# One core, attention and two MLP blocks: attention units of later batches at a lower rank, and the tails of the second block loaded and split earlier

## The chip, the core and the metric

The kernel runs on one NeuronCore of a Trainium2 chip. A core has TensorE (PE, matmuls; its weight loads are listed apart as PEld), VectorE (DVE), ScalarE (ACT), GpSimd (POOL) and SyncE (SP), which issues nearly all of the DMA transfers here. Each engine works through its own list of instructions in the order of the program and waits on semaphores of the others. The metric is the device time of one execution in microseconds (us).

## What is computed

Attention with rotary embedding over 4 batches, 8 heads, 576 positions and head width 64, then an MLP block with a norm, then a gated MLP block. Cut to what matters:

```python
# q, k, v: (4, 8, 576, 64) float32; rotate() is the rotary embedding
q_rot, k_rot = (rotate(q), rotate(k))
scores = scale * np.matmul(q_rot, k_rot.transpose(0, 1, 3, 2))
scores = scores - np.max(scores, axis=-1, keepdims=True)
attn = np.exp(scores)
attn = attn / (np.sum(attn, axis=-1, keepdims=True) + 1e-09)
x = np.matmul(attn, v)                      # then (4, 576, 512)

# first block, d_model 512, hidden 2048
xn = (x - mu) / np.sqrt(var + 1e-06) * g_ln
x = x + np.maximum(xn @ w_ch1, 0.0) @ w_ch2

# second block, d_ff 1024
h = gelu_tanh(x @ w_in)
u, v = (h[..., :512], h[..., 512:])
v_n = (v - mu) / np.sqrt(var + 1e-06) * g_ln
v_s = np.einsum('ts,bsd->btd', w_sg, v_n) + b_sg[None, :, None]
out = x + (u * v_s) @ w_out
```

## The kernel before

**Precision.** A float32 operand is cut into a high and a low part of the fast matmul type, and a product is three matmuls (high by high, low by high, high by low). A cut is a cast on ACT and a subtraction on DVE. The weights of the first block arrive as 8-byte numbers; a "conversion" of one of their 32 tiles is a scaling on ACT (L48), three bit operations on DVE (L50, L52, L55), a cast on ACT (L635) and a subtraction on DVE (L637), and the tile is then stored to a scratch area in DRAM (`wsc`, L641), from which later batches load it again.

**Attention.** The 4 batches follow each other. A batch has 16 units, 64 in all; a unit is one head and 288 of the 576 queries. A unit is: ten score matmuls into `S` (L311, in two parts, four matmuls and six); the maximum over the key chunks on DVE (`mx`, L334); the maximum over partitions on POOL (`am`, L337); then one of two ways to subtract the maximum and exponentiate. Until all 32 converted tiles are stored, five matmuls on PE add minus the maximum into `S` (L392, below "add") and ACT exponentiates out of `S` (L395); afterwards DVE subtracts (L376, `sT<-S,am`, below "subtract") and ACT exponentiates (L381). At last five float32 matmuls with the values (`PV`, L350; the trace shows ten, since each runs as two passes) and two copies on ACT. `S` exists once, so a unit's scores wait for the exponentials of the unit before.

**First block.** Beside the attention of a batch, PE works on the first block of the batch before it: `up` (L655 to L657, 12 matmuls for one output tile) and `down` (L685 to L687). Their results lie in two banks and are evacuated by ACT and DVE (`h`, L663 and L665; `acc`, L699 and L702). Between attention and first block of a batch stands its norm: DVE takes the sums of the exponentials (L477, after their transfer `sums<-sr`, L364), their reciprocal, and then `ln` matmuls on PE (L492, L508, L549) alternate with DVE and ACT. The attention results lie in 17 tiles `x0`, 8 for a batch; so the third batch's units beyond its first two must wait until the first batch's block has stored its result.

**What sets the order.** All of this is written out by a planner (`Sched`). Its tasks are Python generators that name, step by step, an engine, an earliest time and a duration. It takes the step that can start first; a step of lower rank number goes first if it could start within 0.4 of that step's duration. Units had rank 0 (0.5 once their PV runs), evacuations 1, norms 2, preparation of queries, keys and values 3 to 3.2, weight loads 3.5, conversions 4, the first block's matmuls 5. The durations are constants in the code, and the resulting order is fixed in the program.

**Second block** (`moe2`). It takes the batches in turn: `V` (L1006 to L1008, the half that is normed; 5 output tiles for an even batch, since the fifth holds the last 64 positions of two batches, the "tails"), then gelu and norm statistics, the split of the normed tiles (`w<-v`, L1023 and L1025), `U` (L1038 to L1040), the position mixing `G` (L1054 to L1058), and the output (L963 to L965). Its inputs are loaded by `load_x` (L937) and `load_tails` (L977) and split by L949, L951 and, for the tails, L981 and L983. The first batch's loads and splits are tasks of the planner, run while the last first-block work goes on (`ahead`, rank 4.5); everything behind them is ordered by the framework.

Of the kernel before, what the change touches and what calls it, by code (L numbers as in the profile page):

```python
# [20 lines left out]
KEY0 = (0, 128, 256, 384, 448)  # L21
L_CONV = 10.0
HOLD = 0.4
FG = [4, 8, 8, 4]

AHEAD = 2
# [6 lines left out]
def f32(ap):  # L33
    return ap.bitcast(F32)
# [24 lines left out]
class Sched:  # L59
# [27 lines left out]
    def run(self, until=lambda: False):  # L87
        while self.tasks and not until():
# [6 lines left out]
            for x in sorted((x for x in c if x[3]["eng"] == t["eng"] and x[1] < rank), key=lambda x: x[:3]):  # L95
                if x[0] - s < HOLD * t["us"]:
                    s, rank, _, t = x
# [27 lines left out]
def latest(*xs):  # L125

    return None if any(x is None for x in xs) else max(xs)


class Attn:  # L130
# [172 lines left out]
    def unit(self, i):  # L303
        nc, c, u = self.nc, self.c, self.units[i]
        B, j, S, g, p, hi = u["B"], u["j"], self.S, u["g"], u["p"], u["hi"]
        Kb = B["kof"]

        def scores(c0, c1):
            for ch in range(c0, c1):
                for t in range(2):  # L310
                    x = nc.tensor.matmul(S[:, ch, 0:HQ], Kb["K"][j][:, KEY0[ch]:KEY0[ch] + 128], B["X"][:, j, 1 - t, :],  # L311
                                         start=t == 0, stop=t == 1)
                    if ch < 2 and "exp" in self.last:
                        self.tc.declare_no_dep(x.ins, self.last["exp"][1].ins, reason="reads the other banks")

        yield "PE", lambda: latest(self.Sfree[0], Kb["k0"], B["q"][j], self.k["x0_free"](g, p, hi)), 0.55
        scores(0, 2)
        self.Sfree[0] = None
        e = yield "PE", lambda: latest(self.Sfree[1], Kb["k"]), 0.82
        scores(2, 5)  # L320
        self.Sfree[1] = None
        self.k["x0"](g, p, hi)
        B["left"] -= 1
        if B["left"] == 0:
            self.X.give(B["xslot"], e + 0.1)
        Kb["kusers"] -= 1
        if Kb["kusers"] == 0:
            self.K.give(Kb["kslot"], e + 0.1)
        if i + 1 < len(self.units):
            c.task(self.unit(i + 1), 0)  # L330
        self.ahead(i)
        e = yield "DVE", e + 0.35, 1.68
        mx = self.p.tile([128, HQ], F32, tag="mx", name="mx", bufs=1)
        nc.vector.tensor_reduce(mx, S[:, :, 0:HQ].rearrange("p c q -> p q c"), AX.X, ALU.max)  # L334
        e = yield "POOL", e + 0.1, 1.75
        am = self.p.tile([128, HQ], F32R, tag="am", name="am", bufs=AB)
        nc.gpsimd.partition_all_reduce(am, mx, 128, bass_isa.ReduceOp.max)  # L337
        if self.k["spare"]():
            x1, slot, sT = yield from self.subtract(am, e)
        else:  # L340
            x1, slot, sT = yield from self.add(am, e)
        V = B["vof"]
        ps = None
        for c0, c1 in ((0, 2), (2, 5)):
            e = yield "PE", (lambda: latest(x1, self.PV.free(), V["v"])) if c0 == 0 else 0.0, 0.51 * (c1 - c0), 0.5
            if c0 == 0:
                bank = self.PV.take()
                ps = self.ps.tile([128, 512], F32, tag="PV", name="PV")[:, 0:HQ]
            for ch in range(c0, c1):
                nc.tensor.matmul(ps, V["vin"][:, ch, 64 * j:64 * j + 128], sT[:, ch, :], start=ch == 0, stop=ch == 4)  # L350
        self.sT.give(slot, e)
        V["users"] -= 1
        if V["users"] == 0:
            self.vfree.give(V["vslot"], e)
        a, b = 64 * j, 64 - 64 * j
        yield "ACT", e + 0.35, 0.41
        nc.scalar.copy(self.k["x0"](g, p, hi)[a:a + 64], ps[a:a + 64])  # L357
        e = yield "ACT", 0.0, 0.41
        t = self.p.tile([128, HQ], F32, tag="sr", name="sr", bufs=1)
        nc.scalar.copy(t[b:b + 32], ps[b:b + 32])  # L360
        self.PV.give(bank, e + 0.1)
        e = yield "SP", e + 0.1, 0.6
        r = 32 * hi + 2 * p + j
        nc.sync.dma_start(out=self.sums[self.sums_of(g, hi)][r:r + 1], in_=t[b:b + 1])  # L364
        if u["ends"]:
            self.done.append(e + 3.0)
# [57 lines left out]
def fused_kernel(ctx, tc, q, k, v, cs, cst, w12, wi, wo, wsg, wsg4, gb, out):  # L424
# [163 lines left out]
    for g in range(NG):  # L588
        n = FG[g]
        for F in range(16 // n):  # L590
# [53 lines left out]
    def up(g, f, hh):  # L644
# [15 lines left out]
        def end(e=e):  # L660
            e = yield "ACT", e + 0.35, 0.43
            t = h[g, f, hh] = hpool[g].tile([128, 2, HQ], F32R, tag="h", name="h", bufs=FG[g] * 2)
            G["relu"] = nc.scalar.activation(t[:, 0, :], ps, AF.Relu).ins  # L663
# [7 lines left out]
    def down(g, F, c, hh):  # L671
        n = FG[g]
        b, halves = groups[g]
# [45 lines left out]
    def mlp_pass(g, F, halves=(0, 1), ups=None):  # L719

        n = FG[g]
        seq = [(f, hh) for f in ups or range(n) for hh in halves]
# [17 lines left out]
    def open_h(g):  # L740
        if g in hpool:
            return
        if FG[g] != hpool.get("n"):
            if g:
                hpool["ctx"].close()
            hpool["n"], hpool["ctx"] = FG[g], ExitStack()
            hpool[g] = hpool["ctx"].enter_context(tc.tile_pool(name=f"h{g}", bufs=1, side="left"))
# [63 lines left out]
    def last_group():  # L811
        wpool = pctx.enter_context(tc.tile_pool(name="w2b", bufs=1, side="right"))
        pps = pctx.enter_context(tc.tile_pool(name="ps2", bufs=6, space=PS))
        w2.rest(wpool)
        second.append(moe2(tc, M, hpool[NG - 1], wpool, pps, B, x1d, w2.t, gbt, eps, out, lambda: xn[1] == 2 * NG))
# [83 lines left out]
def moe2(tc, M, hp, wpool, pp, B, x1d, w, gbt, eps, out, through):  # L899
# [23 lines left out]

    X = {}

    def load_x(b):
        if b >= B:
            return
        x1, at = {}, {}
        xh, xl = [], []  # L930
        X[b] = (x1, xh, xl)
        for c in range(4):
            for hh in range(2):
                qs = slice(HQ * hh, HQ * hh + HQ)
                e = yield "SP", 0.0, 0.6
                x1[c, hh] = t = M.tile([128, HQ], F32, tag="x0", name="x0", bufs=17)
                nc.sync.dma_start(out=t, in_=x1d[b, c, :, qs])  # L937
                at[c, hh] = e or 0.0
        for c in range(4):
            if c == 2:  # L940
                yield "SP", lambda: 0.0 if through() else None, 0.0
            if c % 2 == 0:
                xh.append(M.tile([128, 2, 576], F32R, tag="xh", name="xh", bufs=2))
                xl.append(M.tile([128, 2, 576], F32R, tag="xl", name="xl", bufs=2))
            for hh in range(2):
                qs = slice(HQ * hh, HQ * hh + HQ)
                t, h, l = x1[c, hh], xh[c // 2][:, c % 2, qs], xl[c // 2][:, c % 2, qs]
                e = yield "ACT", at[c, hh] + 4.0, 0.42
                nc.scalar.copy(h, t)  # L949
                yield "DVE", (e or 0.0) + 0.1, 0.46  # L950
                nc.vector.tensor_tensor(l, t, f32(h), ALU.subtract)  # L951
# [20 lines left out]
    def load_tails(b):  # L972

        s = M.tile([128, 512], F32, tag="sq", name="tails", bufs=2)
        for c in range(4):
            e = yield "SP", 0.0, 0.6
            nc.sync.dma_start(out=s[:, 128 * c:128 * c + 128].rearrange("p (b q) -> p b q", b=2),  # L977
                              in_=x1d[b:b + 2, c, :, 512:576].rearrange("b p q -> p b q"))
        e = yield "ACT", (e or 0.0) + 4.0, 0.63
        tails[b] = t = M.tile([128, 2, 512], F32R, tag="w", name="w", bufs=WB)  # L980
        nc.scalar.copy(t[:, 0, :], s)  # L981
        yield "DVE", (e or 0.0) + 0.1, 0.7
        nc.vector.tensor_tensor(t[:, 1, :], s, f32(t[:, 0, :]), ALU.subtract)  # L983

    def at_once(steps):
        for _ in steps:
            pass

    yield from load_x(0)
    yield from load_tails(0)  # L990
    yield None
    for b in range(B):
        x1, xh, xl = X[b]
# [48 lines left out]
        if b:  # L1042
            final(b - 1)
        at_once(load_x(b + 1))
        if b % 2 and b + 1 < B:
            at_once(load_tails(b + 1))
        gt = {}
        for hh in range(2):
            qs = slice(HQ * hh, HQ * hh + HQ)
            for c in range(4):  # L1050
# [11 lines left out]
                g = gt[c, hh] = hp.tile([128, 2, HQ], F32R, tag="h", name="h", bufs=8)  # L1062
# [66 lines left out]
```

## Time and profile before

| | |
|---|---|
| median of three runs | 999.93 us (998.19 to 1001.24) |
| the profiled execution's own time | 1002.52 us |
| span of its trace, first to last instruction | 1000.7 us |
| PE busy / PEld busy | 939.7 us (94%) / 867.8 us (87%) |
| DVE / ACT / POOL busy | 714.2 (71%) / 444.6 (44%) / 91.4 us (9%) |
| mean granted TensorE clock | 0.985 of full speed |
| chain that ended last | PE 73%, DVE 14%, DMA 5% |

The profiled execution took 1.8 us more than its span and 2.6 us (0.26%) more than the median run. Busy time of an engine counts only executing instructions; what a matmul's end is, the profiler models, so that matmuls overlap in the rows and "busy" PE is not PE at its peak. Times below count from the start of the span.

### The profile page before, as it was taken

How to read it: one execution, taken by the hardware profiler on the slowest of the kernel's cores; microseconds unless marked ns; L12 is line 12 of the kernel's file. 1: busy time of each engine (PE TensorE's matmuls, PEld its weight loads, DVE VectorE, ACT ScalarE, POOL GpSimd, SP SyncE). 2: the span in 40 equal slices, each digit the busy share in tenths (PEclk: the TensorE clock that was granted, in tenths of full speed). 3: DMA queues.
4: the chain of work that ended last, by engine and by line, in shares of the span. 5: the costliest groups of instructions: out<-in, count | busy, mean ns of one | idle time of the engine just before them, and what ended most of it. 6: DMA issues, size and time to landing. Idle time of an engine off the chain costs nothing.

```text
span 1000.7 us, 15881 instructions
## 1 busy us (share of the span) xinstructions
PE 939.7 (94%) x6057; PEld 867.8 (87%) x6057; DVE 714.2 (71%) x1188; ACT 444.6 (44%) x901; POOL 91.4 (9%) x78
## 2 busy tenths in 40 slices
PE   4688899999998889999999999999999979999998
PEld 3566688798898778989998999999999969989998
DVE  6998666699788788865589744586553887667764
ACT  3564554665434355443235531425222546345441
POOL 1121112122000211100012110000000000000000
PEclk9899999999999899999999999999999989999999
DMA  9888444378464564653755533588763300303011
GB/s 273 240 283 263 110 106 109 104 202 258 152 207 146 189 213 134 204 163 121 251 182 145 156 128 127 192 285 273 250 204 91 90 1 12 95 2 89 1 49 48
DMA packets 93420, 153.76 MB, mean 154 GB/s; under 512 B 38048, under 2 KB 60576, under 8 KB 93344
## 3 DMA queue, kind: packets, MB, share of 16 engines
q1 hardware_dynamic: 92800, 152.16, 49.1%
q8 instruction: 48, 0.79, 0.3%
q10 hardware_dynamic: 544, 0.59, 0.2%
q14 instruction: 28, 0.23, 0.1%
HBM read 107.25 MB, written 26.21 MB: 133 GB/s over the span
## 4 chain that ended last, share of the span: by engine, by line
PE 73%; DVE 14%; DMA 5%; ACT 2%; issue 2%; POOL 2%; SPq 1%; DVEq 0%; ACTq 0%; POOLq 0%
PE PV L350 8%; PE S L311 7%; PE m L686 6%; PE m L685 6%; PE m L687 6%; PE m L655 5%; PE m L657 5%; PE m L656 5%; DVE mx L334 4%; DMA sums<-sr 3%; PE S L392 2%; PE p L1054 2%; PE p L1055 2%; PE p L1056 2%; DVE sT L376 2%
## 5 line engine op out<-in xcount | busy, mean ns | idle before, releaser
L350 PE MATMUL PV<-sT,vin 128*128 128x288 f32 x640 | 170.8, 413 | 3.6 <-ACT sr L360 1.8
L655 PE MATMUL m<-xh,w 128*128 128x288 f32 x480 | 148.0, 308 | 2.4 <-DVE h L665 2.3
L350 PEld LDWEIGHTS PV<-sT,vin 128*128 128x128 f32 x640 | 120.1, 194 | 32.7 <-ACT sr L360 2.7
L685 PE MATMUL m<-h,w 128*128 128x288 f32 x480 | 145.2, 302 | 0.0
L686 PE MATMUL m<-h,w 128*128 128x288 f32 x480 | 142.0, 296 | 0.0
L334 DVE TENSOR_REDUCE mx<-S 128x288 f32<-128x1440 f32 x64 | 106.0, 1657 | 49.9 <-PE S L311 48.8
L656 PE MATMUL m<-xl,w 128*128 128x288 f32 x480 | 141.5, 295 | 0.0
L657 PE MATMUL m<-xh,w 128*128 128x288 f32 x480 | 141.2, 294 | 0.0
L687 PE MATMUL m<-h,w 128*128 128x288 f32 x480 | 140.5, 293 | 0.0
L337 POOL PARTITION_ALL_REDUCE am<-mx x64 | 89.3, 1395 | 500.4 <-DVE mx L334 500.4
L311 PE MATMUL S<-X,K 128*128 128x288 f32 x640 | 112.6, 321 | 16.8 <-ACT X L200 10.2
L311 PEld LDWEIGHTS S<-X,K 128*128 128x128 f32 x640 | 95.5, 201 | 29.2 <-ACT sT L395 11.0
L665 DVE SCALAR_TENSOR_TENSOR h<-m,h 128x288 fp32r<-128x288 f32 x128 | 58.0, 454 | 66.6 <-ACT h L663 65.8
L655 PEld LDWEIGHTS m<-xh,w 128*128 128x128 f32 x480 | 90.0, 188 | 6.5 <-DVE h L665 3.6
L663 ACT ACTIVATE h<-m 128x288 fp32r<-128x288 f32 x128 | 52.2, 408 | 95.0 <-PE m L657 94.5
L656 PEld LDWEIGHTS m<-xl,w 128*128 128x128 f32 x480 | 90.2, 188 | 1.4
L686 PEld LDWEIGHTS m<-h,w 128*128 128x128 f32 x480 | 90.2, 188 | 1.0
L685 PEld LDWEIGHTS m<-h,w 128*128 128x128 f32 x480 | 90.0, 188 | 1.1
L657 PEld LDWEIGHTS m<-xh,w 128*128 128x128 f32 x480 | 90.3, 188 | 0.0
L687 PEld LDWEIGHTS m<-h,w 128*128 128x128 f32 x480 | 90.2, 188 | 0.0
L357 ACT COPY x<-PV 64x288 f32<-64x288 f32 x64 | 25.2, 394 | 137.8 <-PE PV L350 137.7
L395 ACT ACTIVATE sT<-S 128x576 f32<-128x576 f32 x74 | 53.6, 769 | 29.7 <-PE S L392 28.3
(149 smaller groups left out, 1848.9 us busy)
## 6 DMA issues: line engine op xcount, KB each, us to landing
w<-wsc SPq DMA_DIRECT2D x96, 512.0 KB, 4.3
X<-qin SPq DMA_DIRECT2D x124, 144.0 KB, 2.6
cd<-in_w SPq DMA_DIRECT2D x32, 512.0 KB, 6.1
wsc<-w SPq DMA_DIRECT2D x24, 512.0 KB, 3.6
qin<-in_q SPq DMA_DIRECT2D x31, 288.0 KB, 4.4
kin<-in_k SPq DMA_DIRECT2D x15, 576.0 KB, 5.0
vin<-in_v SPq DMA_DIRECT2D x40, 160.0 KB, 4.2
x1d<-x SPq DMA_DIRECT2D x32, 144.0 KB, 2.7
```

Of the source, the lines that this page charges most:

```text
L311: x = nc.tensor.matmul(S[:, ch, 0:HQ], Kb["K"][j][:, KEY0[ch]:KEY0[ch] + 128], B["X"][:, j, 1 - t, :], start=t == 0, stop=t == 1)
L334: nc.vector.tensor_reduce(mx, S[:, :, 0:HQ].rearrange("p c q -> p q c"), AX.X, ALU.max)
L337: nc.gpsimd.partition_all_reduce(am, mx, 128, bass_isa.ReduceOp.max)
L350: nc.tensor.matmul(ps, V["vin"][:, ch, 64 * j:64 * j + 128], sT[:, ch, :], start=ch == 0, stop=ch == 4)
L395: ex.append(nc.scalar.activation(sT[:, c0:c1, :], self.S[:, c0:c1, 0:HQ], AF.Exp, scale=0.125))
L655: nc.tensor.matmul(ps, w[:, 0, ms], xh[:, kc, :], start=kc == 0, stop=False)
L656: nc.tensor.matmul(ps, w[:, 0, ms], xl[:, kc, :], start=False, stop=False)
L657: nc.tensor.matmul(ps, w[:, 1, ms], xh[:, kc, :], start=False, stop=kc == 3)
L665: nc.vector.scalar_tensor_tensor(t[:, 1, :], ps, 0.0, f32(t[:, 0, :]), op0=ALU.max, op1=ALU.subtract)
L685: nc.tensor.matmul(ps, w[:, 0, ms], t[:, 0, :], start=a == 0, stop=False)
L686: nc.tensor.matmul(ps, w[:, 1, ms], t[:, 0, :], start=False, stop=False)
L687: nc.tensor.matmul(ps, w[:, 0, ms], t[:, 1, :], start=False, stop=a == n - 1)
```

## The change

Two edits. First, a unit of batch 1, 2 or 3 (counted from 0) enters the planner with rank 2.5 and no longer 0, so its scores, maximum, subtraction and exponentials stand behind evacuations (1) and norms (2) where these could start at about the same time. Units of batch 0 keep rank 0. Second, `load_tails` is cut into the loads (`load_tails`) and the split (`split_tails`); for the first batch of the second block the tails are loaded before the other inputs, and split in the middle of `load_x`, ahead of the two last chunks. For the third batch nothing changes: both halves run at once, as before.

```diff
+UNIT = (0, 2.5, 2.5, 2.5)
...
         if i + 1 < len(self.units):
-            c.task(self.unit(i + 1), 0)
+            c.task(self.unit(i + 1), UNIT[self.units[i + 1]["g"]])
...
-    def load_x(b):
+    def load_x(b, between=()):
...
             if c == 2:
                 yield "SP", lambda: 0.0 if through() else None, 0.0
+                yield from between
...
         s = M.tile([128, 512], F32, tag="sq", name="tails", bufs=2)
+        e = None
         for c in range(4):
...
+        return s, e
+
+    def split_tails(b, s, e):
         e = yield "ACT", (e or 0.0) + 4.0, 0.63
...
-    yield from load_x(0)
-    yield from load_tails(0)
+    s = yield from load_tails(0)
+    yield from load_x(0, split_tails(0, *s))
     yield None
...
         if b % 2 and b + 1 < B:
-            at_once(load_tails(b + 1))
+            at_once(split_tails(b + 1, *at_once(load_tails(b + 1))))
```

By its new ranks the planner writes another order for PE, DVE, ACT and SP from the 17th unit on, the first of the second batch; POOL's is the same. Six units fewer use the add (31, before 37) and six more the subtract (33, before 27), since the 32 conversions are now through earlier in the order. All other instructions keep their number. (Line numbers of the changed kernel are one higher up to the second block, and some nine higher in it.)

Second batch, DVE. All that stands from the maximum of the 28th unit to the one after it, before (`mx` the maximum, `qin` a query split, `ce` and `w<-ce` conversion steps):

```order
L334 TENSOR_REDUCE mx<-S 128x288
L202 TENSOR_TENSOR qin<-qin 128x288
L55 SCALAR_TENSOR_TENSOR ce<-cd,ce 128x512
L50 TENSOR_SCALAR ce<-ce 128x512
L52 SCALAR_TENSOR_TENSOR ce<-cd,ce 128x512
L637 TENSOR_TENSOR w<-ce,w 128x512
L55 SCALAR_TENSOR_TENSOR ce<-cd,ce 128x512
L334 TENSOR_REDUCE mx<-S 128x288
```

The same place on DVE in the changed kernel (`h<-m,h` evacuates a bank of the first block):

```order
L335 TENSOR_REDUCE mx<-S 128x288
L666 SCALAR_TENSOR_TENSOR h<-m,h 128x288
L203 TENSOR_TENSOR qin<-qin 128x288
L666 SCALAR_TENSOR_TENSOR h<-m,h 128x288
L51 TENSOR_SCALAR ce<-ce 128x512
L53 SCALAR_TENSOR_TENSOR ce<-cd,ce 128x512
L56 SCALAR_TENSOR_TENSOR ce<-cd,ce 128x512
L666 SCALAR_TENSOR_TENSOR h<-m,h 128x288
L638 TENSOR_TENSOR w<-ce,w 128x512
L51 TENSOR_SCALAR ce<-ce 128x512
L53 SCALAR_TENSOR_TENSOR ce<-cd,ce 128x512
L56 SCALAR_TENSOR_TENSOR ce<-cd,ce 128x512
```

Between two maxima stand now eleven other instructions where six stood: more of the conversions and of the first block's evacuations fall to one unit. On PE a unit of this batch goes with 36 matmuls of the first block, before with 18.

Third batch, PE. The start of its third and fourth unit before (`S<-X` scores, `S<-am` the add):

```order
L311 MATMUL S<-X,K_1936 128x288 x10
L392 MATMUL S<-am,e_63 128x288 x5
L311 MATMUL S<-X,K_1937 128x288 x10
L350 MATMUL PV<-sT,vin_81 128x288 x5
L392 MATMUL S<-am,e_63 128x288 x5
```

The same start on PE in the changed kernel (`ln` belongs to the second batch's norm, `m<-h` is `down` work):

```order
L312 MATMUL S<-X,K_2368 128x288 x4
L509 MATMUL ln<-lt,ones 128x288
L312 MATMUL S<-X,K_2368 128x288 x6
L686 MATMUL m<-h,wx 128x288
L687 MATMUL m<-h,wx 128x288
L688 MATMUL m<-h,wx 128x288
```

Before, nothing stood between the scores and the add that needs their maximum. Now 126 `down`, `up` and `ln` matmuls stand between these scores and the fourth unit's, and there is no add: this unit subtracts on DVE.

Second block, DVE. Around the split of the first tails before (`acc` and `x` end the last batch's first block, `sq` and `acc<-sq` are gelu steps of `U`):

```order
L920 SCALAR_TENSOR_TENSOR sq<-sq,acc 128x288
L922 SCALAR_TENSOR_TENSOR acc<-sq,acc 128x288
L710 TENSOR_TENSOR x_5540<-acc,x_5540 128x288
L983 TENSOR_TENSOR w<-tails,w 128x512
L920 SCALAR_TENSOR_TENSOR sq<-sq,acc 128x288
```

The same split on DVE in the changed kernel (`xl<-x,xh` is the split of the other inputs):

```order
L953 TENSOR_TENSOR xl<-x_7438,xh 128x288
L953 TENSOR_TENSOR xl<-x_7440,xh 128x288
L666 SCALAR_TENSOR_TENSOR h<-m,h 128x288 x2
L989 TENSOR_TENSOR w<-tails,w 128x512
L953 TENSOR_TENSOR xl<-x_7442,xh 128x288
L666 SCALAR_TENSOR_TENSOR h<-m,h 128x288
```

The split moved from behind the last batch's final additions to a place ahead of the last inputs' split. On PE the fifth `V` tile's 12 matmuls moved with it: before, 8 `U` matmuls stood between the last of them and the first `G` matmul; now 95 `U` and 24 `down` matmuls stand there.

## Rows read from the trace of the kernel before

**Rows 1.** First part of the page: busy us, share, instructions of each engine.
```profile
PE 939.7 (94%) x6057; PEld 867.8 (87%) x6057; DVE 714.2 (71%) x1188; ACT 444.6 (44%) x901; POOL 91.4 (9%) x78
```
**Rows 2.** Stretches: length, busy us (instructions) of PE PEld DVE ACT POOL, clock, DMA share, GB/s.
```profile
164.30:200.50 36.20, 34.00 (x191) 28.79 (x190) 23.47 (x30) 22.92 (x43) 7.11 (x6) 1.00 0.33 89
200.50:256.70 56.20, 55.98 (x346) 50.50 (x345) 50.28 (x69) 35.55 (x69) 12.90 (x9) 1.00 0.80 243
256.70:322.00 65.30, 63.66 (x464) 62.11 (x463) 56.47 (x116) 27.24 (x55) 1.10 (x1) 1.00 0.45 154
...
334.00:380.80 46.80, 43.74 (x260) 37.51 (x259) 36.97 (x46) 22.30 (x41) 7.97 (x7) 1.00 0.69 221
...
803.00:814.00 11.00, 3.76 (x15) 3.44 (x15) 10.53 (x25) 8.62 (x19) 0.00 (x0) 0.70 0.00 1
```
**Rows 3.** Timeline of PE, third batch's start and second batch: start, us, [idle before].
```profile
327.48 1.57 PE L392 MATMUL S<-am,e 128*128 128x288 f32 x5 [4.18 <-POOL am L337]
329.06 2.77 PE L311 MATMUL S<-X,K 128*128 128x288 f32 x10
331.63 3.19 PE L350 MATMUL PV<-sT,vin 128*128 128x288 f32 x10
...
251.78 0.82 PE L392 MATMUL S<-am,e 128*128 128x288 f32 x5
...
253.24 1.56 PE L311 MATMUL S<-X,K 128*128 128x288 f32 x10
254.63 2.59 PE L350 MATMUL PV<-sT,vin 128*128 128x288 f32 x10
```
**Rows 4.** Short stretches, same columns: third batch's start, and the second block.
```profile
328.00:330.00 2.00, 1.98 (x9) 1.63 (x7) 1.97 (x5) 1.73 (x4) 0.00 (x0) 0.50 0.00 0
...
814.00:820.00 6.00, 6.00 (x47) 6.00 (x46) 3.81 (x8) 0.87 (x2) 0.00 (x0) 0.99 0.00 0
```
**Rows 5.** Timelines of DVE, PE and ACT around the first G matmul of the second block.
```profile
795.74 0.69 DVE L983 TENSOR_TENSOR w<-tails,w 128x512 fp32r<-128x512 f32 x1
...
801.55 0.39 PE L1008 MATMUL p<-wih,w 128*128 128x512 f32 x1
...
809.57 3.34 ACT L1023 CAST w<-v 128x512 fp32r<-128x512 f32 x6 [0.84 <-DVE v L1019]
...
810.24 1.81 PE L1054 MATMUL p<-wgh,w 128*128 128x288 f32 x6 [7.24 <-ACT w L1023]
```
**Rows 6.** Groups of DVE instructions by line: busy us, mean ns, idle us before.
```profile
L334 DVE TENSOR_REDUCE mx<-S 128x288 f32<-128x1440 f32 x64 | 106.0, 1657 | 49.9 <-PE S L311 48.8 <-ACT qin L200 0.9
L665 DVE SCALAR_TENSOR_TENSOR h<-m,h 128x288 fp32r<-128x288 f32 x128 | 58.0, 454 | 66.6 <-ACT h L663 65.8
L376 DVE TENSOR_TENSOR sT<-S,am 128x1440 f32<-128x1440 f32 x27 | 44.6, 1650 | 9.2 <-POOL am L337 9.0
L52 DVE SCALAR_TENSOR_TENSOR ce<-cd,ce 128x512 int32<-128x512 int32 x44 | 31.7, 720 | 0.9
```
**Rows 7.** Timelines of DVE (one row) and POOL, second batch: start, us.
```profile
164.09 1.35 DVE L176 TENSOR_TENSOR kin<-kin,csb 128x1152 f32<-128x1152 f32 x1
...
164.26 2.19 POOL L337 PARTITION_ALL_REDUCE am<-mx  x1 [5.94 <-DVE mx L334]
...
200.48 1.15 POOL L337 PARTITION_ALL_REDUCE am<-mx  x1 [6.87 <-DVE mx L334]
...
256.65 1.15 POOL L337 PARTITION_ALL_REDUCE am<-mx  x1 [5.35 <-DVE mx L334]
```
**Rows 8.** Second batch's norm on DVE, and the transfer of the sums it needs.
```profile
258.54 0.30 DVE L477 TENSOR_SCALAR sum<-sums 64x288 f32<-64x288 f32 x1 [1.98 <-DMA wsc<-wx]
...
DMA to landing us min/median/max: 1.6/2.1/8.4
```
**Rows 9.** PE's waits for the maximum, whole span, then first batch: us, times, longest.
```profile
PE S L392 <- POOL am L337: 22.2, 14, 4.2
...
PE S L392 <- POOL am L337: 17.3, 11, 3.8
```

More of the change, by code (lines that the diff above doesn't have):

```diff
@@ L985, in at_once @@
     def at_once(steps):
-        for _ in steps:
-            pass
-    yield from load_x(0)
-    yield from load_tails(0)
+        while True:
+            try:
+                next(steps)
+            except StopIteration as x:
+                return x.value
+    s = yield from load_tails(0)
+    yield from load_x(0, split_tails(0, *s))
     yield None
```

## The prediction

> **What bounds the kernel now.** I read the page's busy times first, then the stretches, then, for the stretches in which PE is not full, the timelines, and last the groups by line. PE is busy for 94% of the span [rows 1]; so the question for an edit that moves instructions is where the other 6%, some 61 us, lie, and whether the moved work gets there. About half of that is in the first batch's attention (up to 136 us), which keeps its rank and its order. What the edits can reach lies in five places. In 803 to 814 PE does 3.76 us of work in 11 [rows 2]: the first G matmul waits 7.24 us for the split of the normed tiles [rows 5], and the clock is down behind that. At 327.48 an add waits 4.18 us for its maximum [rows 3], and again the matmuls after it run at half clock: 0.50 in 328 to 330, against 0.99 in 814 to 820 [rows 4]. In 164.3 to 200.5, 256.7 to 322 and 334 to 380.8 PE is idle for 2.2, 1.6 and 3.1 us (length minus busy) [rows 2]. The stretch of 200.5 to 256.7 shows the other thing to be seen: PE is full (0.2 us idle) while DVE is at 50.28 of 56.2, 89%, and DMA at 0.80 [rows 2]. That is what an even mixture of scores, conversions and first block costs, and it is what the second batch will look like throughout.
>
> **The change part by part.** The sum is made against the profiled execution, 1002.52 us, whose span is 1000.7.
>
> Six adds become subtracts. An add is five matmuls. At full clock 47 matmuls take 6.00 us [rows 4], 0.128 each, so 30 fewer save 3.8 us; by the longer figure of a whole add, 0.82 [rows 3], they would save 4.9. The subtracts put 6 times 1.65 us on DVE [rows 6], 9.9 us, at the end of the second batch and the start of the third. DVE is at 79% in 334 to 380.8 and at 86% in 256.7 to 322 [rows 2], so some 19 us are free there; they hide it. If DVE were full there, the 9.9 us would be paid.
>
> The tails. Before, the fifth V tile waited until DVE split the tails at 795.74, and its last matmul came at 801.55; from there to the first G matmul at 810.24 [rows 5] the chain of gelu, statistics, square root and split runs 8.7 us, with only 8 U matmuls to cover it. Now 119 matmuls stand there in the order, 119 x 0.128 = 15.2 us, and the chain fits in. ACT has the evacuation of U in the same list; the six casts took 3.34 us [rows 5], and with the two copies of each U tile and the table loads between I estimate some 11 us there, still below 15.2. So the wait of 7.24 goes. The clock follows: in 803 to 814 PE ran 15 matmuls in 3.76 us [rows 2]; at 0.128 they take 1.9, so 1.9 are gained. Together 9.1. The four tail loads pass eight input loads on SP; a transfer issue there is under half a us, and the splits are placed behind evacuations that wait for PE anyway, so I cost the move at nothing. If U's evacuation held ACT and DVE longer than 15.2 us, some of the 7.24 would return at G's banks; I put the bounds of this part at 4 and 9.1.
>
> The third batch's start. Scores, maximum, then the add: nothing stood between on PE. Now 126 other matmuls do, 16 us, and the unit's subtract and exponentials have these for cover. The 4.18 us go. Of the half clock behind it, the add took 1.57 for 0.82, the scores 2.77 for 1.56 and the PV 3.19 for 2.59 [rows 3]: 2.6 us more. Together 6.8; bounds 2 (the wait moves to another unit) and 6.8.
>
> The second batch. In 164.3 to 200.5 six units ran [rows 7] with little first-block work beside them, because the norms of the first batch stood behind these units' steps; now the norms go first and the work is there two units earlier. The idle time is 2.2 us, but matmuls that wait between passes count as busy. The weight loads show that: PEld is busy 28.79 of 36.2 there and 37.51 of 46.8 in 334 to 380.8, 80% in both, and 90% where PE is full, in 200.5 to 256.7 [rows 2]. At 90% the two stretches would last 32.0 and 41.7 us, 4.2 and 5.1 less; by the idle time alone 2.2 and 3.1. Part of the lower share comes from PV and norm matmuls, which stream longer for each load, so I take the middle, 3.2 and 4.1. The Trainium skill ("Perfetto Trace Analysis", Identifying Performance Opportunities) says that matmul busy time is a bad measure of the distance to the limit and the weight loads' share a good one; by it the two would be 4.2 and 5.1, and the sum 2.0 us lower. Of the 1.6 us in 256.7 to 322, short waits of the norm for its neighbours, I take half, 0.8, since the norm is now spread among more matmuls.
>
> What it costs. In the dense stretch a unit takes (256.65 - 200.48)/8 = 7.02 us [rows 7]. Its PE work by the order is 33 matmuls at 0.128 and ten PV passes at twice that, 6.78; so 0.24 is lost for each. Now a unit of the second batch has 51 and ten, 9.1 us, and on DVE, from the rows between two maxima (the maximum 1.66, bit operations 0.72, evacuations 0.45 [rows 6]), 7.9 to some 10 us, about 8.8 in the mean: full, but not over. Six units that did not have this loss get it: 6 x 0.24 = 1.4. The other side: the second batch's norm ranks before units, so DVE, which is in order, stands at the sums' transfer with a unit's maximum queued behind. It waited 1.98 us there before, and a sums transfer lands after 2.1 us in the median and 8.4 at the longest [rows 8]. I take 1.0, with 0 and 6 as bounds.
>
> The sum: 3.8 + 9.1 + 6.8 + 3.2 + 4.1 + 0.8 = 27.8 gained, 1.4 + 1.0 = 2.4 paid, 25.4 net. 1002.5 - 25.4 = 977.1. The median of the runs is 0.9974 of the profiled execution (999.93/1002.52), which gives 974.6 us for the median after.
>
> **The rivals.** (a) POOL and DVE get in each other's way in the second batch. At 164.09 DVE began a multiplication with two inputs in SBUF (kin by csb, 1.35 us), and the all-reduce that began at 164.26 took 2.19 us, where others take 1.15 [rows 7]: it was held for about a us. In the second batch nearly all that DVE does beside the maxima are such operations or short evacuations. If every unit of the 14 with conversions beside it loses that 1.04, 14.6 us are paid, and the median is 989.2. The Trainium skill ("SBUF — State Buffer", Who interferes with whom) has a DVE instruction with two SBUF inputs and a GpSimd instruction that reads SBUF exclude each other, whichever came second waiting for all of the first. By that rule the time comes out as this rival has it, as far as the chain is uncovered. Against it: the order puts an evacuation with one SBUF input right behind most maxima now, and about 30 first-block matmuls, 3.8 us, between scores and add, which cover 1.7 + 1.15 with a us to spare. (b) The second block's stall stays: G waits for U's evacuation or its banks, where it waited for the split. The 9.1 come back: 983.7. For it speaks that ACT and DVE are both nearly full in 803 to 814 [rows 2]; against it, that the cover is twice the chain. (c) Only tails and adds pay, and the first-block work moved ahead leaves a hole of the same size later: 3.8 + 9.1 = 12.9, so 989.6, or 987 in the median. (d) Slower: DVE becomes the bound of the second batch, in one way: a maximum that finds conversions and evacuations ahead of it comes late, and the add behind it stops PE with all that is queued. Before, PE waited 22.2 us in 14 such waits, 4.2 at the longest, and 17.3 us of it in the first batch, where DVE does conversions beside scores [rows 9]. It decides from 2.0 us a unit (27.8/14); at 4.2 for each of 14 the cost is 58.8, and the median 1002.5 + 58.8 - 27.8 = 1033.5, less 2.6: 1031. (e) That the change does little of what it says, since a rank decides only between steps that could start at nearly the same time: the orders exclude that, PE's differs from the 17th unit to the end of the first block.
>
> **How the numbers follow.** The forecast has 0.60, (a) 0.16, (b) 0.08, (c) 0.07, a cancellation of (a), (b) and the sums' wait to within 0.3% (about what a measurement of this kernel can tell from no change) 0.04, and (d) 0.05. Around 974.6 the costs reach up by 0 to 5 more for the norm and some of (a); down by 1.1 (adds), 2.0 (weight loads), 0.8 and 2.4 (costs at nothing), 6 in all, and 4 to 5 more if the 0.24 a unit shrinks. The range of 963 to 990 takes in the forecast and (a), (b) and (c), and leaves out the rest. Faster by over 0.3% (below 997) has 0.90, the same 0.05, slower 0.05.
>
> **What would show it.** In the trace after: the first G matmul of the second block starts without a wait and the clock stays at 1.00 through it; the add of the third batch's third unit is gone, and the half clock with it; units of the second batch stand 9.2 to 9.6 us apart on POOL, with PE idle under 2%. Wrong if these units stand over 10.5 us apart with PE waiting for the maximum (a, d), if PE waits for the sums or the norm for over 5 us near the second batch's end, or if a wait of 5 us stands at G under another name (b).

## The result

The changed kernel takes 975.68 us in the median (975.26 to 977.34), the kernel before, run beside it, 1000.46: a ratio of 0.976, 95% interval 0.974 to 0.978. The forecast was 974.6. The profiled execution took 977.34 us with a span of 975.6. A second measurement on another chip, shown below, gives 0.975 (0.973 to 0.978).

Two executions of the same instructions can differ by some 4 us in the first batch's attention, which neither edit touches. So stretches are compared below from the start of the 16th all-reduce on POOL (one all-reduce a unit, so the first batch's last; it began at 128.5 us in both profiles) to the last instruction: 872.2 us before and 847.1 after, **25.1 gained where the sum said 25.4**. The first part of the page after, against [rows 1]:

```profile
PE 928.8 (95%) x6027; PEld 861.5 (88%) x6027; DVE 722.4 (74%) x1194; ACT 445.7 (46%) x901; POOL 88.1 (9%) x78
```

Two stretches hold the gain: from the 16th all-reduce to the last unit's, and from there to the end. The columns are those of [rows 2]; first the kernel before, whose rows of these stretches were not shown yet:

```profile
128.50:591.30 462.80, 448.66 (x2860) 410.30 (x2859) 356.79 (x503) 219.04 (x430) 65.51 (x48) 0.99 0.55 168
591.30:1000.70 409.40, 397.75 (x2790) 384.51 (x2788) 253.58 (x546) 159.24 (x351) 1.15 (x1) 0.99 0.35 113
```

The same two stretches of the changed kernel:

```profile
128.50:580.50 452.00, 444.39 (x2866) 410.26 (x2865) 366.31 (x509) 222.21 (x432) 62.10 (x48) 1.00 0.57 174
580.50:975.60 395.10, 390.62 (x2754) 378.00 (x2752) 252.46 (x546) 157.47 (x349) 1.15 (x1) 1.00 0.35 115
```

The first stretch lost 10.8 us, though six more matmuls run in it (36 of the first block more, 30 of the adds fewer); the second lost 14.3, of which the 36 matmuls that left it are 36 times 0.133, 4.8. PE's idle time fell from 14.1 to 7.6 us in the first and from 11.7 to 4.5 in the second. In the first stretch the weight loads took the same time in both kernels, 410.3 us, so their share rose with the shorter stretch, from 88.7% to 90.8%; PE's busy time fell by 4.3 us for as many matmuls. This is the point of the Trainium skill ("Perfetto Trace Analysis", Identifying Performance Opportunities) that was weighed ahead: busy time of matmuls misses a part of the distance to the limit, here 4.3 of 10.8 us, that the weight loads' share shows. Not all of the 4.3 is density: the half clock cost 2.6 us in this stretch before, by the prediction's rows, and 1.4 now, as told below, so 1.2 of it is the clock.

Shorter stretches of the changed kernel, in the same columns: the second batch, its end with the third batch's start, two pieces of that, the third batch, and the second block around its first `G` matmul:

```profile
136.00:287.80 151.80, 150.15 (x977) 139.47 (x976) 129.35 (x191) 85.31 (x163) 19.66 (x16) 1.00 0.62 200
287.80:330.00 42.20, 39.02 (x255) 36.93 (x254) 36.75 (x71) 14.30 (x30) 2.31 (x2) 0.96 0.47 146
...
322.00:326.00 4.00, 1.00 (x8) 0.78 (x7) 3.53 (x9) 0.87 (x2) 0.00 (x0) 1.00 0.23 76
326.00:330.00 4.00, 4.00 (x20) 4.00 (x20) 3.53 (x9) 1.28 (x3) 0.00 (x0) 0.57 0.00 0
...
330.00:443.30 113.30, 112.56 (x711) 102.24 (x710) 88.76 (x95) 56.97 (x110) 21.02 (x16) 1.00 0.55 162
...
776.00:800.00 24.00, 24.00 (x183) 24.00 (x182) 21.00 (x52) 18.13 (x45) 0.00 (x0) 1.00 0.11 32
```

PE is idle for 1.7 us in 151.8 in the second batch and 0.7 in 113.3 in the third. Only one hole is left, 287.8 to 330 with 3.2 us, and three of them lie in 322 to 326, with the clock at 0.57 behind. On DVE and PE (timelines: start, us, idle before in brackets) this hole is a step of the second batch's norm:

```profile
322.66 0.46 DVE L703 TENSOR_TENSOR acc<-m,acc 128x288 f32<-128x288 f32 x1 [0.37 <-PE m L688]
323.15 0.46 DVE L709 TENSOR_TENSOR acc<-acc,rstd 128x288 f32<-128x288 f32 x1
323.64 0.46 DVE L711 TENSOR_TENSOR x<-acc,x 128x288 f32<-128x288 f32 x1
324.02 0.45 DVE L501 TENSOR_TENSOR lt<-x,x 128x288 f32<-128x288 f32 x1
324.38 0.94 DVE L529 SCALAR_TENSOR_TENSOR xl<-xc,gbt,xh 128x288 fp32r<-128x288 f32 x2
325.24 0.45 DVE L495 TENSOR_TENSOR x<-ln,x 128x288 f32<-128x288 f32 x1
...
322.46 0.29 PE L493 MATMUL ln<-rc,sel 128*128 128x288 f32 x1
325.75 0.40 PE L493 MATMUL ln<-rc,sel 128*128 128x288 f32 x1 [3.00 <-DVE x L495]
```

The `ln` matmul at 325.75 needs the bank that L495 empties on DVE, and DVE comes to it only after six other instructions in a row, three of them the last additions of the first batch's block (`acc`, `x`). On PE nothing stands between this `ln` matmul and the one at 322.46. All the waits of PE for the maximum and for this step, over the whole span (us, times, longest), against [rows 9]:

```profile
PE ln L493 <- DVE x L495: 3.4, 3, 3.0
...
PE S L393 <- POOL am L338: 17.2, 12, 3.8
```

The 17.2 us lie almost wholly in the first batch, where it was 17.3 before; the 4.2 at the third batch's start are gone. Against [rows 7], the first batch's last all-reduce, the second batch's first and its two last, with the DVE instruction that one of them began behind:

```profile
128.50 1.15 POOL L338 PARTITION_ALL_REDUCE am<-mx  x1 [5.93 <-DVE mx L335]
138.21 1.15 POOL L338 PARTITION_ALL_REDUCE am<-mx  x1 [8.56 <-DVE mx L335]
...
270.65 0.45 DVE L703 TENSOR_TENSOR acc<-m,acc 128x288 f32<-128x288 f32 x1
270.83 1.15 POOL L338 PARTITION_ALL_REDUCE am<-mx  x1 [8.12 <-DVE mx L335]
280.08 1.15 POOL L338 PARTITION_ALL_REDUCE am<-mx  x1 [8.09 <-DVE mx L335]
```

From the 16th to the 32nd, (280.08 - 128.50)/16 = 9.47 us lie between two units in the mean; single gaps go from 9.1 to 11.4. Against [rows 5], the second block's start, on DVE, PE and ACT:

```profile
750.29 0.69 DVE L989 TENSOR_TENSOR w<-tails,w 128x512 fp32r<-128x512 f32 x1
...
771.01 0.39 PE L1017 MATMUL p<-wih,w 128*128 128x512 f32 x1
...
783.16 1.68 ACT L1032 CAST w<-v 128x512 fp32r<-128x512 f32 x3
...
787.08 0.43 PE L1063 MATMUL p<-wgh,w 128*128 128x288 f32 x2
```

The tails are split 45 us earlier, the last `V` matmul starts at 771.01, and the first `G` matmul follows at 787.08 without a wait (no bracket), where 7.24 us stood. Before, it began behind the first of the six casts (809.57 + 0.64, one cast, is 810.21). That first cast now ends near 783.8, 3.3 us ahead of the matmul, so 12.8 of the 16.1 us of cover are used. The last cast ends at 787.09, and DVE's part of the fourth tile's split at 788.42, while `G` already runs; PE shows no gap there (24.00 of 24 us busy in 776 to 800).

### The profile page after: what moved, and what is told of

Same layout as the page of the kernel before. It is cut to its first block, busy times and chain, and to the rows that moved or that the text cites. A ratio compares the mean times of both kernels' runs of the same rounds, so it can differ in the third digit from the quotient of the medians.

```text
span 975.6 us, 15819 instructions
## 1 busy us (share of the span) xinstructions
PE 928.8 (95%) x6027; PEld 861.5 (88%) x6027; DVE 722.4 (74%) x1194; ACT 445.7 (46%) x901; POOL 88.1 (9%) x78
## 4 chain that ended last, share of the span: by engine, by line
PE 84%; DVE 9%; DMA 2%; ACT 2%; issue 2%; POOL 1%; SPq 0%; DVEq 0%; ACTq 0%
PE PV L351 12%; PE S L312 8%; PE m L687 7%; PE m L686 7%; PE m L688 7%; PE m L656 6%; PE m L658 6%; PE m L657 6%; DVE mx L335 2%; PE p L1047 2%; PE p L1049 2%; PE p L966 2%; PE p L1048 2%; PE p L1064 2%; PE p L965 2%; PE p L1065 2%
## 5 line engine op out<-in xcount | busy, mean ns | idle before, releaser
L312 PE MATMUL S<-X,K 128*128 128x288 f32 x640 | 114.4, 321 | 18.3 <-ACT X L201 10.2
L338 POOL PARTITION_ALL_REDUCE am<-mx x64 | 85.9, 1343 | 492.9 <-DVE mx L335 492.9
L312 PEld LDWEIGHTS S<-X,K 128*128 128x128 f32 x640 | 96.0, 199 | 29.3 <-ACT X L201 10.2
L666 DVE SCALAR_TENSOR_TENSOR h<-m,h 128x288 fp32r<-128x288 f32 x128 | 58.0, 453 | 54.9 <-ACT h L664 54.2
L377 DVE TENSOR_TENSOR sT<-S,am 128x1440 f32<-128x1440 f32 x33 | 54.5, 1651 | 18.2 <-POOL am L338 18.1
```

Source lines behind the costliest of these rows:

```text
L377: nc.vector.tensor_tensor(sT, self.S[:, :, 0:HQ], f32(am).unsqueeze(1).to_broadcast([128, NC5, HQ]), ALU.subtract)
L666: nc.vector.scalar_tensor_tensor(t[:, 1, :], ps, 0.0, f32(t[:, 0, :]), op0=ALU.max, op1=ALU.subtract)
```

## The experiments

The theory: the edits act apart from each other. The tails give some 9 us by covering one chain; the rank gives the rest, because evacuations and norms that go first leave matmuls of the first block to stand between a unit's scores and what needs its maximum. Rivals were that the adds, the POOL chain or another batch carry it. Diffs are against the changed kernel. "From 16th" is the time from the 16th all-reduce to the last instruction in the profile; before it is 872.2.

| kernel | median us | ratio to before (95%) | from 16th, us |
|---|---|---|---|
| changed | 975.68 | 0.976 (0.974 to 0.978) | 847.1 |
| after_again | 976.59 | 0.975 (0.973 to 0.978) | 847.2 |
| tails_only | 991.78 | 0.990 (0.989 to 0.992) | 863.0 |
| units_only | 984.66 | 0.983 (0.981 to 0.985) | 855.1 |
| six_adds | 973.64 | 0.972 (0.971 to 0.974) | 845.6 |
| pool_twice | 984.54 | 0.984 (0.982 to 0.986) | 857.3 |
| adds_34 | 973.92 | 0.973 (0.971 to 0.976) | 845.7 |
| adds_64 | 989.86 | 0.989 (0.986 to 0.992) | 862.0 |
| batch1_only | 984.22 | 0.982 (0.980 to 0.985) | 856.0 |
| batch12_only | 976.47 | 0.975 (0.973 to 0.978) | 848.2 |
| batch23_only | 994.98 | 0.993 (0.990 to 0.996) | 861.7 |
| behind_evac | 979.27 | 0.977 (0.975 to 0.980) | 850.1 |
| all_adds34 | 1011.93 | 1.011 (1.009 to 1.013) | 845.1 |

**tails_only and units_only: each edit alone.**

```diff
-UNIT = (0, 2.5, 2.5, 2.5)
+UNIT = (0, 0, 0, 0)
```

> The second edit alone: tails loaded first and split in the middle of the other inputs, all units at rank 0 as before. The prediction's theory: the stall of the first G matmul (7.24 us) and the half clock behind it (1.9) go and nothing else does, so 9.1 us under the kernel before: about 991.4, the third batch's add still waits 4.2 us. Rival 1: G waits for something else, less than 4 us gained: 996.5 or more. Rival 2: the two edits overlap, and this one alone already gives over 13 us: below 987.

```diff
-    s = yield from load_tails(0)
-    yield from load_x(0, split_tails(0, *s))
+    yield from load_x(0)
+    s = yield from load_tails(0)
+    yield from split_tails(0, *s)
```

> The first edit alone: units of later batches at rank 2.5, tails loaded and split in the old order. The theory: all but the tail part stays, so the time is the changed kernel's 975.7 plus 9.1, about 984.8, with 7 us idle at the first G matmul and the clock at half behind it. If the new order of units already hid that stall, about 976.

Both came out as the theory has it: 9.2 and 17.1 us from the 16th all-reduce on, 26.3 together, where both edits at once give 25.1; the 1.2 between is not explained. The tails' part can be read by itself, from the last unit's all-reduce to the end: 409.4 to 399.9 us with the old ranks, 404.6 to 395.1 with the new, 9.5 both times. Each kernel keeps the other's stall. With the tails alone PE waits for the maximum as before:

```profile
PE S L393 <- POOL am L338: 23.5, 14, 4.2
```

With the units alone the wait of the first `G` matmul is there in its old size:

```profile
PE p L1064 <- ACT w L1033: 7.2, 1, 7.2
```

**six_adds: the six units keep their add.**

```diff
-        if self.k["spare"]():
+        if self.k["spare"]() and i >= 37:
```

> The changed kernel, but the units 31 to 36 (counted from 0) use the add on PE again, as in the kernel before: 30 matmuls more on PE, six subtracts fewer on DVE (9.9 us). The theory (PE is the bound there and DVE has room): 30 x 0.128 = 3.8 us more, about 979.5. Rival: DVE is the bound at the end of the second batch, so PE's extra work costs nothing and the relief of DVE may gain: 975.7 or less.

The theory's first term fell here. With 30 matmuls more the kernel is faster, by 1.5 us in its stretches and by 2.9 in the ratios to before (0.9723 against 0.9752 for after_again). The stretch from 287.8, in the columns of [rows 2], and PE's waits in 280 to 330 us show where:

```profile
287.80:330.00 42.20, 40.16 (x276) 37.59 (x275) 35.58 (x75) 14.07 (x30) 2.31 (x2) 1.00 0.48 145
```

```profile
PE ln L550 <- DVE h L666: 0.9, 1, 0.9
PE m L657 <- DVE xl L529: 0.8, 1, 0.8
PE ln L493 <- DVE x L495: 0.3, 1, 0.3
```

The wait of 3.0 us for L495 is down to 0.3, no other over 0.9 has come, the clock stays at 1.00, and 276 matmuls run where 255 did.

**adds_34: only the last three of the six, those of the third batch, subtract.**

```diff
-        if self.k["spare"]():
+        if self.k["spare"]() and i >= 34:
```

> The changed kernel, but the last three units ahead of the second batch's norm (31 to 33, counted from 0) use the add on PE; the others are as in the changed kernel. New theory, from the six adds that made it faster where 3.8 us more were expected: these units' subtracts (1.65 us each on DVE) stand among the steps of the second batch's norm, whose ln matmul waits 3.0 us on PE for DVE and lowers the clock; without them 3.0 + 1 to 1.5 go and 15 x 0.128 = 1.9 come: 2 to 3 us under the changed kernel. Rival (PE is the bound there, as the prediction had it): 1.9 us over it.

1.4 us less in the stretches and 2.1 in the ratios, whose intervals overlap; so the size is within what these runs can tell, and the rival, 1.9 slower, falls. The wait is gone in this kernel too, and its longest there is again `PE ln L550 <- DVE h L666` with 0.9 us. The same two `ln` matmuls, on PE:

```profile
316.78 0.30 PE L493 MATMUL ln<-rc,sel 128*128 128x288 f32 x1
...
320.57 0.40 PE L493 MATMUL ln<-rc,sel 128*128 128x288 f32 x1 [0.31 <-DVE x L495]
```

DVE does six instructions between the first of them and the L495 that the second waits for, as many as in the changed kernel. But 24 `down` matmuls, 3.2 us, stand between the two on PE here, and none there. So the wait went because PE's order had work left to cover this step, not because DVE had less to do in front of L495. Without the three subtracts the planner writes the norm's steps earlier in the order; by which of its durations it does so, no run shows. The subtracts in the second batch's last unit and in the third batch's first two, beside the norm, are the ones that don't pay: keeping the other three adds as well (six_adds) changes 0.1 us.

**adds_64: every unit adds.** This prices an add where nothing on DVE is short.

```diff
-        if self.k["spare"]():
+        if self.k["spare"]() and i >= 64:
```

> The changed kernel with the add in all 64 units: 33 x 5 = 165 matmuls more on PE than the changed kernel, 54 us less on DVE. If an add costs its PE time in the third and fourth batch, where PE is full and DVE at 78%, 165 x 0.128 = 21 us more, less the 4 to 5 us of the norm's place: 16 to 21 over the changed kernel. If DVE's 1.65 a unit counts as much there too: within 8 us of it.

33 adds more cost 14.9 us in the stretches and 13.3 in the medians, a little under the 16 to 21 expected. In this sum are the 1.5 us that the adds at the norm gain. Away from it the price has to be read against the kernels that have these adds already: 862.0 - 845.6 = 16.4 us for 27 adds over six_adds, 16.3 for 30 over adds_34, 0.61 and 0.54 each; five matmuls at 0.128 are 0.64. So in the dense stretches a subtract is worth nearly all of the add's PE time, and at the second batch's norm less than nothing.

**pool_twice: the all-reduce of each second-batch unit runs twice**, so the chain from maximum to add is longer by a known time.

```diff
-        nc.gpsimd.partition_all_reduce(am, mx, 128, bass_isa.ReduceOp.max)
+        for _ in range(2 if g == 1 else 1):
+            nc.gpsimd.partition_all_reduce(am, mx, 128, bass_isa.ReduceOp.max)
```

> The changed kernel with the all-reduce of each of the second batch's 16 units done twice on POOL, into the same tile, in an order otherwise the same: 1.15 us more between a unit's maximum and its add. The theory: about 30 first-block matmuls (3.8 us) between the last scores and the add cover 1.66 + 1.15 with about a us to spare, so the cost is under 0.3 us a unit: 976 to 980. Rival (a) of the prediction, that this chain is what times a unit: 1.15 x 16 = 18 us more, about 994.

It missed the 976 to 980 of the theory and landed between it and the rival, 10.2 us above the changed kernel. The rows of POOL (two executions each) and PE's wait for the maximum over the span:

```profile
134.49 2.95 POOL L339 PARTITION_ALL_REDUCE am<-mx  x2 [8.56 <-DVE mx L335]
...
276.73 2.84 POOL L339 PARTITION_ALL_REDUCE am<-mx  x2 [7.38 <-DVE mx L335]
```

```profile
PE S L394 <- POOL am L339: 26.5, 27, 3.8
```

The 16 pairs took 2.40 to 2.95 us, 2.62 in the mean, where one took 19.66/16 = 1.23 in the changed kernel. So 1.4 us were added to each chain, and 10.2/16 = 0.64 of it came through: 0.75 were covered beyond what the single all-reduce needs. PE now waits 27 times in place of 12. The forecast's "a us to spare" was thus 0.75 in the mean, and of rival (a)'s 1.04 a unit, had it come, some 0.3 would have been paid.

**batch1_only, batch12_only, batch23_only: whose rank carries it.** The rank 2.5 for the second batch alone, for second and third, and for third and fourth.

```diff
-UNIT = (0, 2.5, 2.5, 2.5)
+UNIT = (0, 2.5, 0, 0)
```

> Rank 2.5 for the second batch's units alone, the third and fourth back at 0, tails as in the changed kernel. The prediction put all of the units' gain at places that the second batch's order makes (norm and fill in it, the third batch's start, the conversions through earlier): within 3 us of the changed kernel. Rival: the later batches' own ranks carry a third or more of the 17 us: 6 us or more over it.

```diff
-UNIT = (0, 2.5, 2.5, 2.5)
+UNIT = (0, 2.5, 2.5, 0)
```

> Rank 2.5 for the second and third batch, the fourth back at 0; tails as changed. The PE order is the changed kernel's up to the fourth batch, so the third batch's start has its cover. Theory: the 7.6 us that the second batch's rank alone lacked come from the third batch's rank at its own start, so this is within 2 us of the changed kernel: 975 to 979. Rival: the fourth batch's rank carries a share: 980 or more.

```diff
-UNIT = (0, 2.5, 2.5, 2.5)
+UNIT = (0, 0, 2.5, 2.5)
```

> Rank 2.5 for the third and fourth batch's units, the second back at 0; tails as in the changed kernel. With the second batch's units first, the first-block work (16 up and 9 down tiles ahead of the 34th unit's scores, where the changed kernel has 26 and 24) and the conversions stay late, so the third batch starts without cover as in the kernel before (4 us of PE work between the third and the fourth unit's scores, 18 in the changed kernel). Theory: little beyond the tails' part, 988 to 992. Rival: the later batches' ranks carry their 7 to 8 us by themselves: about 984.

The first missed: it is 8.9 us above the changed kernel in the stretches, not within 3. Its third batch starts with a stall again (PE's timeline, and a stretch in the columns of [rows 2]):

```profile
324.00 2.77 PE L312 MATMUL S<-X,K 128*128 128x288 f32 x10 [5.04 <-DVE sT L377]
```

```profile
320.00:330.00 10.00, 6.00 (x18) 5.07 (x19) 8.56 (x13) 3.52 (x7) 2.48 (x2) 0.66 0.39 118
```

It is a wait for a subtract, not for an add's maximum, a little longer than the 4.18 of [rows 3], with the clock at 0.66 over the ten us. With the third batch's rank too (batch12_only) 7.8 of the 8.9 are back, and the fourth batch's gives 1.1, which the medians (976.47 against 975.68 and 976.59) don't show. The third run shows that the second batch's rank is needed for that: without it the other two give 863.0 - 861.7 = 1.3 us over the tails alone. Even 1.3 may be too much: the profile is one of the two short executions of five (989.5 to 996.1), and the median, 994.98, lies above the 988 to 992 expected and above tails_only. From tails_only the gain is thus 7.0 for the second batch, 7.8 for the third on top of it, 1.1 for the fourth.

**behind_evac: units behind evacuations, ahead of norms.**

```diff
-UNIT = (0, 2.5, 2.5, 2.5)
+UNIT = (0, 1.5, 1.5, 1.5)
```

> Rank 1.5 for units of the later batches: behind evacuations (1), ahead of norms (2). Tells the two apart. If the norms' going first is what pays (work for PE comes two units earlier, cover at the third batch's start), most of the units' 17 us is lost: 985 or more. If the evacuations' going first pays: within 3 us of the changed kernel. From the order (second batch filled as in the changed kernel, 6 us of PE work between the third batch's third and fourth scores, 18 in the changed kernel) I expect between: 980 to 984.

3.0 us above the changed kernel, at the border between the two cases, with a median 0.7 under the 980 to 984 expected: of the 15.9 us over tails_only, 12.9 come already with the evacuations first. What the norms' place adds stands at the third batch's scores, which wait here as they do not in the changed kernel:

```profile
PE S L312 <- DVE sT L377: 4.8, 3, 3.1
```

**all_adds34: the first batch's units get the rank too** (on adds_34).

```diff
-UNIT = (0, 2.5, 2.5, 2.5)
+UNIT = (2.5, 2.5, 2.5, 2.5)
...
-        if self.k["spare"]():
+        if self.k["spare"]() and i >= 34:
```

> A try for a faster kernel: rank 2.5 for the first batch's units too, and the add in the three units ahead of the second batch's norm. The first batch's last units get first-block work between them (3 up tiles by the 13th unit, none before), where PE waits for maxima: 2 to 4 us under the variant with three adds alone, 970 to 972. Rival: conversions and norms delay the first batch, whose units are timed by DVE: no gain or a loss.

The rival held. From the 16th all-reduce on it is adds_34 again, 845.1; ahead of it the first batch takes 37 to 40 us longer (its 16th all-reduce begins at 165.2 us, against 128.5 in the changed kernel and 124.7 in adds_34). PE's wait for the maximum over the span, and DVE's waits in the first 170 us:

```profile
PE S L393 <- POOL am L338: 40.4, 15, 4.1
```

```profile
DVE mx L335 <- PE S L312: 21.9, 13, 3.5
DVE mx L335 <- ACT sr L361: 13.3, 2, 7.5
```

In adds_34 these are 19.5 us for PE and, in the first 126 us, 7.9 for DVE's wait for scores. No first-block matmul runs before 121.8 us, and of the 40 us 33 are lost by the 12th all-reduce (130.3 us, against 97.3 in adds_34). So what goes ahead of a unit there is not matched by matmuls that could fill PE. The low rank itself gains nothing; it pays where other matmuls stand ready.

**after_again: the changed kernel once more**, on the chip of adds_34.

> The changed kernel itself, beside the next three on one chip. Expected at 0.976 of the kernel before, 975 to 978.

It repeats to 0.1 us in the stretches, and the same wait of 3.0 us for L495 stands in it, so that wait belongs to the order and not to one execution.

## Why the prediction held, and which terms did not

The total is right, 25.4 against 25.1, and so are the two mechanisms. Of the single terms two were wrong, one of them in its sign: some 5 us were lost at the second batch's norm that the sum did not have, and 4.6 more than forecast came elsewhere. That the total fits to 0.3 us is luck.

- **The tails: 9.1 forecast, 9.5 measured**, in two pairs of kernels. The steps are as told: no wait at `G`, clock 1.00 in 776 to 800. The margin was smaller than told: the chain to the first cast's end took 12.8 us where I estimated some 11, under a cover of 16.1 where I had 15.2. So 3.3 us were left, and the "twice the chain" that I set against rival (b) was 1.26 times. That ACT is nearly full in 803 to 814, which spoke for it, was read too high: 8.62 of 11 us are 78%.
- **The third batch's start: 6.8 forecast.** The add, its wait and the half clock behind it are gone. batch1_only, which brings a stall of that kind back, stands 8.9 us higher. This is a bound from a kernel whose whole third batch is ordered otherwise, not a measurement of the term. The step "nothing stood between on PE; now 126 other matmuls do" holds; that the third batch's own rank was needed for it I had not said, and in batch1_only I expected it of the second batch's.
- **Six adds: 3.8 gained by the forecast; 1.5 lost by six_adds** (2.9 by the medians' ratios). The failed step is "some 19 us are free there; they hide it". The free time of DVE was taken from shares over 47 and 65 us. A share over such a stage says nothing of one step: at the norm's last `ln` matmuls PE waits for six DVE instructions in a row, and in the order that comes with the subtracts no matmul is left to cover them, where adds_34 has 24. The forecast named the price if DVE were full there, 9.9 us; what came through was the 3.8 not gained and these 1.5, some 5.
- **The norm: 1.0 taken, with 0 and 6 as bounds; 4.4 measured**, 3.0 of wait and 1.4 of clock (13 matmuls from 326.39 to 329.51 at 0.24 us in place of 0.133). Not for the sums' transfer, as the step had it: no wait for it appears there. PE waits for L495 with nothing left to run; in adds_34 the same DVE work stands there under 24 matmuls, and the wait is 0.31. This loss and that of the six adds are one event, so they are not to be added up.
- **The second batch: 3.2 + 4.1 + 0.8 less 1.4.** With six_adds' 26.6 us and the tails' 9.5 taken off, 17.1 are left for the third batch's start, the density and the norm together; the forecast had 6.8 + 3.2 + 4.1 + 0.8 - 1.4 - 1.0 = 12.5. So 4.6 more came than was summed. By the weight loads' share, which was the upper of the two measures (4.2 and 5.1), it would have been 14.5; the middle was the worse choice. The remaining 2.6 I cannot assign. One count was off: from 164.26 to 200.48 lie five units, not six, so the cost of 1.4 would have been 1.2; and the chances of the single outcomes add up to 0.91 for faster and 0.04 for the same, where the line has 0.90 and 0.05.
- **The spacing: 9.2 to 9.6 us forecast, 9.47 measured**, with PE idle for 1.1% of the second batch where under 2% was named. The rivals (c), (d) and (e) are excluded by that, by units_only, and by PE's waits for the maximum after the first batch, 0.6 us in one place.
- **Rival (a)** did not occur: twelve of the second batch's sixteen all-reduces took 1.15 us and POOL's busy time in the 16 went down, from 24.7 us before to 19.7. The order was the reason given, and the runs agree: in tails_only and batch23_only, whose second batch has the old rank, the 16 take 24.7 us again, three of them 2.19, and in units_only and batch1_only 19.7. Ten of the twelve short ones began behind the evacuation of a bank (L666, L703, L495), the other two while DVE did nothing. What this is worth in time no run shows; 5.0 us are 0.31 a unit, less than the 0.75 that pool_twice found covered.

A faster kernel than both is the changed one with the adds kept in front of the second batch's norm: 0.972 and 0.973 against 0.975 for the changed kernel. The medians and the stretches agree on the sign for both; the intervals overlap or touch, so the 1.5 to 3 us are likely, not settled.

## What to carry to other kernels

Where an in-order engine is said to hide moved work, its free share over a stage doesn't tell: look at each instruction that another engine waits for, and at what that other engine still has to run meanwhile. Six DVE instructions in a row cost PE 3.0 us with nothing beside them and 0.31 with 24 matmuls. Letting evacuations go ahead of the stage that needs a long chain pays where other matmuls are ready to fill the time (15.9 us in three batches), and can cost more than that where none are (37 to 40 in one); so give such a rank stage by stage. A stall that has been covered should be reported with the margin that is left, since the next edit will use it.

## What the hardware showed that I had not expected

- One wait of 3.0 us cost 4.4. The clock stood at 1.00 in 322 to 326, with PE busy for 1.00 of the 4 us, and fell only with the matmuls that followed, to 0.57 over 326 to 330, near the lower of its two levels, 1.2 of 2.4 GHz. Behind the waits of up to 0.9 us in six_adds the stretch stayed at 1.00.
- The all-reduce's time varies with what stands beside it: single ones took 1.15 to 2.19 us in the second batch before, 1.15 to 1.71 after, and pairs 2.40 to 2.95 in pool_twice. What stood beside a long one is always as in [rows 7]: each of the ten over 2 us in the two traces, seven before and three after, began 0.17 to 0.26 us after a `kin<-kin,csb` multiply of 1.35 us on DVE.
- DVE's free time did hide moved work away from the norm: there an add's five matmuls, 0.64 us of PE, cost 0.54 to 0.61 when they came back (adds_64 against adds_34 and six_adds), so hardly any of it is lost on the longer path over DVE.
